# Attention probabilities turned by VectorE in 32x32 blocks and regrouped by transfers inside SBUF, in place of 128x128 transposes on TensorE

## The chip, the cores and the metric

The kernel runs on one core of a Trainium2 chip. The metric is the device time of one execution in microseconds (us), the median of several runs. A profiled execution gives a trace with the start and duration of every instruction. The engines are called PE (TensorE), DVE (VectorE), ACT (ScalarE), POOL (GpSimd) and SP (SyncE, which here issues most DMAs). Each takes its own list of instructions in order and waits on semaphores for the others.

## The reference

Block-causal attention for 8 batches of 8 heads (576 rows, head size 64, blocks of 64 rows), then a bilinear feed-forward layer over all 4608 tokens:

```python
scores = scale * np.matmul(q, k.transpose(0, 1, 3, 2))
mask = block_i >= block_j                      # blocks of 64
scores = np.where(mask, scores, -1000000000.0)
scores = scores - np.max(scores, axis=-1, keepdims=True)
attn = np.exp(scores)
attn = attn / (np.sum(attn, axis=-1, keepdims=True) + 1e-09)
x = np.matmul(attn, v)                         # heads side by side: 4608 x 512
out = ((x @ w_a) * (x @ w_b)) @ w_out          # 512 -> 1536 -> 512
```

All data is float32 (the large products run as three float32r products of high and low parts).

## The kernel before, in words

**Pairs and slots.** The 64 heads are worked in 32 pairs, and the program is a loop over slots `s` (line 576). In slot `s` three generators are advanced by the table `SLOT` (line 572): `softmax` (`S_`) of pair `s`, `turn` (`T_`) of pair `s-1`, and `values` (`V_`) of pair `s-2`, which stands first in the slot. After each step some matmuls of the first feed-forward pass (`first_pass`, called MoE matmuls below, 128x288) are put in to keep PE fed: 72 in a slot, shared out by the third numbers of the entries. They begin in slot 5. In slots 0 to 4 filler matmuls (`keep`) stand there, and the conversion of the weights (lines 141 to 212) runs on DVE and ACT.

**One pair.** The queries of a head are four tiles of 128 rows, `t` = 0 to 3, against 192, 320, 448 and 512 keys, plus a small side product for the first and the last block of queries (`e_s`, 128x128 per head). `softmax` makes the scores on PE (line 383): first tile 3, the side and tile 1, then in a second batch tiles 2 and 0. DVE takes the maxima (line 388; the two 512-wide ones of tile 3 come first in a pair), ACT the exponentials with their sums (line 391). When all are there, DVE forms the reciprocals `rc` (lines 429 to 434) and POOL scales the exponentials by them in place (line 438, ten instructions: four of tiles 3 and 2, two of the side, four of tiles 1 and 0).

**The turn.** The product with `v` needs the probabilities with the keys on the partitions. `turn` transposes them on PE against an identity (line 457), 28 transposes of 128x128 a pair into PSUM, four at a time, and ACT copies each four to SBUF (`ah`, line 460, 7 copies a pair). `values` then multiplies by `v` (line 475, `av`): per head 6 matmuls over up to 512 query columns, the two heads of the pair in the two halves of the array. DVE copies the result out (lines 484 and 485), ACT and POOL split it into high and low parts (`xh`, `xl`), and ACT's queue stores it.

**What sets the order.** PE's order is the program's order, since the loop stands in a manual schedule for PE. On the other engines the framework's scheduler decides it, so it is read from the compiled instruction lists. Of the slot's other work, the split of the next query and key into high and low parts (`q` on ACT and DVE, `k` on ACT, line 112, and POOL, line 115), and the parts of the feed-forward (`a`, `hf`, `hh`, `hl`, `ob`) share the engines.

**Buffers.** The exponentials have two sets of buffers (two pairs). PSUM has 8 banks: 2 for the MoE matmuls, 4 for scores (`ps_sc`), 2 for `tp` and `av` (`ps_t`).

Of the kernel before, what the change touches and what calls it, by code (L numbers as in the profile page):

```python
# [8 lines left out]

F32 = mybir.dt.float32  # L10
# [7 lines left out]
P = 128  # L18
BLK = 64
# [12 lines left out]
XQ = lambda nc: nc.scalar  # L32
PE_ORDER = ["PE"]
WARM = 9
KEEP = [3, 1, 1, 1, 1]
NATIVE = 6

# [17 lines left out]
def attention_then_bilinear_ffn(  # L55
# [10 lines left out]
    nc = tc.nc  # L66
    B, H, D, S = kT.shape
# [23 lines left out]
    left, right = ExitStack(), ExitStack()  # L91
# [18 lines left out]
    def split(hi, lo, src, hi_eng, lo_eng):  # L110
        if hi_eng is nc.scalar:
            nc.scalar.copy(hi, src)  # L112
        else:
            hi_eng.tensor_copy(hi, src)
        return lo_eng.tensor_tensor(lo, src, f32(hi), op=ALU.subtract)
# [43 lines left out]
    def parts(fs):  # L159
        return [(f, i) for f in fs for i in range(KP)] + [(f, KP) for f in fs]  # L160
# [53 lines left out]
    marks = []  # L214
# [72 lines left out]
    SC = slice(P * SIDE_T, P * SIDE_T + BLK), slice(P * SIDE_T + BLK, P * (SIDE_T + 1))  # L287
# [15 lines left out]

    if WARM:
        z = const.tile([P, W], F32R, name="z")
        nc.vector.memset(f32(z), 0.0)
        ps = ps_mm.tile([P, 512], F32, tag="mm", name="warm")
        for k in range(WARM):
            nc.tensor.matmul(ps, z[:, :P], z, start=True, stop=True)

    heads = {}
    xs_all = {}

    def pair_of(p):
        b, h = divmod(2 * p, H)
        return b, h, f"{b}_{h}"
# [10 lines left out]
    def load_qk(p):  # L327

        b, h, n = pair_of(p)
        take(p, "k", S, kT[b, h:h + 2].rearrange("h d s -> (h d) s"))  # L330
        take(p, "q", SQ, qT[b, h:h + 2].rearrange("h d s -> (h d) s"))

    def load_v(p):
        b, h, n = pair_of(p)
        vv = heads[p]["v"] = apool.tile([P, 2, NCH + 1, D], F32, tag="v", name=f"v{n}", bufs=3)
        for j in range(2):
            nc.sync.dma_start(vv[:, j], vm[b, h + j])
# [19 lines left out]
    rows = slice(D), slice(D, P)  # L357
# [83 lines left out]
    def turn(p):  # L441

        n = pair_of(p)[2]
        heads[p]["a"] = ah = apool.tile([P, 2, NCH, W], F32, tag="ah", name=f"ah{n}")
        for t, hs in [(t, [h]) for t in range(LAST, 0, -1) for h in range(2)] + [(0, [0, 1])]:
            tp = ps_t.tile([P, 4, P], F32, tag="tp", name=f"tp{n}_{t}_{hs[0]}", bufs=2)
            m = min(t + 2, NCH)
            todo = []
            for h in hs:
                es, e_s = e_bufs[(2 * p + h) % NE]  # L450
                todo += [es[t][:, c * P:(c + 1) * P] for c in range(m)]
                if t == SIDE_T:
                    assert m == SIDE
                    todo.append(e_s)
            m = len(todo) // len(hs)
            for c, src in enumerate(todo):
                mark = nc.tensor.transpose(tp[:, c], src, ident)  # L457
            at = slice(hs[0], hs[-1] + 1), slice(m), slice(P * t, P * (t + 1))
            got = tp[:, :len(todo)].rearrange("p (h c) n -> p h c n", h=len(hs))
            nc.scalar.copy(ah[(slice(None), *at)], got)  # L460
            yield mark

    def values(p):

        b, h, n = pair_of(p)
        t = heads.pop(p)
        hp = h // 2
        xf = xpool.tile([P, S], F32, tag="xf", name=f"xf{n}", bufs=XFB)
        av = ps_t.tile([P, W], F32, tag="tp", name=f"av{n}", bufs=2)
        av0 = ps_t.tile([P, 512], F32, tag="tp", name=f"av0{n}", bufs=2)[:, :BLK]  # L470
        v, a = t["v"], t["a"]

        def both(out, c, src, cols, start, stop):
            for i, r in enumerate(rows):
                mark = nc.tensor.matmul(  # L475
                    out[r], v[:, i, c], a[:, i, src, cols], start=start, stop=stop, skip_group_check=True)
# [5 lines left out]
        both(av[:, W - BLK:], NCH, SIDE, SC[1], False, True)  # L482
        mark = both(av0, NCH, SIDE, SC[0], True, True)
        nc.vector.tensor_copy(xf[:, BLK:], av)  # L484
# [64 lines left out]
    NP = NH // 2  # L549
    LAG = 2  # L550
# [8 lines left out]
    def want(now):  # L559

        n = (now - H - LAG) * per_slot - behind
        if now < 2 * H + LAG:
# [13 lines left out]
    for s in range(NP + LAG):  # L576
        if s == NP - 1:
            raw = fetch(wab[F1, :, 0], f"w{F1}_0")
        due = 0
        for k, (what, i, m) in enumerate(SLOT):  # L580
            i += s
            if 0 <= i < NP:
                mark = next(gens.get((what, i)) or gens.setdefault((what, i), what(i)))
                for _ in range(KEEP[s] if s < len(KEEP) else 0):
                    keep = keep or ps_mm.tile([P, 512], F32, tag="mm", name="keep")
                    nc.tensor.matmul(keep, z[:, :P], z, start=True, stop=True)  # L586
                marks.append(mark)
            if k == 0 and s < NP:
                load_v(s)
            if k == 9 and s + 1 < NP:  # L590
                split_qk(s + 1)
            if k == 9 and s + 2 < NP:
# [12 lines left out]
            while moe and n_moe < want(now):  # L605
                next(moe)
                n_moe += 1
# [146 lines left out]
    k = 0  # L754
# [8 lines left out]
    for kp in range(KP):  # L763
        g = sums_x(raw, kp, "0_0")
# [5 lines left out]
    start, pace = F2 * PER_F, STEP1  # L770
    k = 0


    for ps_ in range(2):
        fs = list(range(F1 + ps_ * F2, F1 + (ps_ + 1) * F2))
        for tt in range(NT2):
# [21 lines left out]
            todo = [(j, o) for j in (1, 0) for o in range(NO)]  # L798
            hs = {}
# [75 lines left out]
```

## Time and profile before

| | |
|---|---|
| time, median of 3 runs | 1277.9 us (1276.22 to 1278.17) |
| the profiled execution | 1277.34 us, of which the span that the trace covers is 1275.5 us |
| attention with MoE matmuls | about 110 to 660 us of the span |
| rest of the first pass, then two passes over four and four feed-forward blocks | from 660 us on |
| PE transposes (line 457) | 896 a kernel, 28 a pair |
| copies `ah` (line 460) | 224, mean 597 ns, 133.5 us of ACT |

Busy time is not the bound by itself: it says how long an engine had instructions running. To see what sets the time one asks in each stage which engine never waits, and for an engine that waits, what ends the wait. Lines of a timeline give a start, a duration, the engine and line, what is written and read, and in brackets the idle time before it and what ended it.

### The profile page before, as it was taken

What the parts mean: (1) busy time and instruction counts of PE and PEld (TensorE: products, weight loads), DVE (VectorE), ACT (ScalarE), POOL (GpSimd) and SP (SyncE); (2) the same over time, 40 slices, a digit from 0 to 9 for tenths busy, and PEclk for the clock granted to TensorE, in tenths of its full rate; (3) what the DMA queues carried; (4) which work ended last, traced back from release to release, by engine and by line L of the source; (5) the groups of instructions that cost most, each with busy time, mean ns of one, the idle gap of its engine ahead of it and who ended that gap; (6) DMA issues with size and microseconds to landing.
All of it is one profiled execution on the core that took longest, in us unless ns stands there. A gap on an engine that the chain in (4) does not pass through costs nothing.

```text
span 1275.5 us, 22228 instructions
## 1 busy us (share of the span) xinstructions
PE 1229.0 (96%) x8132; PEld 1114.6 (87%) x8132; DVE 789.1 (62%) x1932; ACT 622.8 (49%) x1550; POOL 353.5 (28%) x540
## 2 busy tenths in 40 slices
PE   6789999999999999999999899999999999999998
PEld 4556778888888888888889799999999999999998
DVE  5875444345444454444538999778778677577664
ACT  3656667576675665766645444344344223123210
POOL 2453653554535545355330020120121000000000
PEclk7888999999999999999999999999999999999999
DMA  5342222222222223221133454563578542253131
GB/s 191 107 139 72 71 77 81 96 65 74 80 88 88 65 73 97 70 88 59 35 109 95 151 119 135 153 153 95 142 192 278 161 149 85 65 149 102 47 100 62
DMA packets 68652, 135.66 MB, mean 106 GB/s; under 512 B 7616, under 2 KB 42432, under 8 KB 68544
## 3 DMA queue, kind: packets, MB, share of 16 engines
q1 hardware_dynamic: 57024, 115.37, 28.2%
q0 software_dynamic: 6912, 9.44, 4.7%
q10 hardware_dynamic: 4608, 9.44, 2.2%
q8 instruction: 64, 1.05, 0.3%
q14 instruction: 44, 0.36, 0.1%
HBM read 87.03 MB, written 47.19 MB: 105 GB/s over the span
## 4 chain that ended last, share of the span: by engine, by line
PE 74%; ACT 12%; DVE 10%; issue 3%; DMA 1%; POOL 0%; SPq 0%; ACTq 0%; DVEq 0%
PE pso_z L727 15%; PE ps L223 9%; PE psw_z L681 8%; PE psx_z L681 8%; PE psv_z L681 7%; PE av L475 7%; PE pso L223 6%; PE tp L457 5%; PE s L383 5%; ACT e L391 5%; ACT ah L460 4%; PE psy_z L681 4%; DVE nm L388 3%; ACT e_s L391 2%; PE keep L586 1%
## 5 line engine op out<-in xcount | busy, mean ns | idle before, releaser
L223 PE MATMUL ps<-xh,wab 128*128 128x288 f32 x1024 | 228.8, 305 | 0.0
L727 PE MATMUL pso_z<-h_z,wo 128*128 128x384 f32 x1152 | 203.7, 334 | 2.1 <-DVE u_z L708 2.1
L727 PEld LDWEIGHTS pso_z<-h_z,wo 128*128 128x128 f32 x1152 | 200.2, 188 | 2.5 <-issue 2.3
L438 POOL TENSOR_SCALAR e<-e,rc 128x512 f32<-128x512 f32 (+3 forms) x256 | 150.7, 611 | 161.4 <-DVE rc L434 95.2
L223 PEld LDWEIGHTS ps<-xh,wab 128*128 128x128 f32 x1024 | 168.1, 188 | 8.5 <-issue 5.2
L223 PE MATMUL ps<-xl,wab 128*128 128x288 f32 x512 | 158.0, 309 | 0.0
L460 ACT COPY ah<-tp 128x512 f32<-128x512 f32 x224 | 133.5, 597 | 41.6 <-PE tp L457 41.1
L388 DVE TENSOR_REDUCE nm<-s 128x1 f32<-128x512 f32 (+4 forms) x320 | 147.0, 484 | 9.1 <-PE s L383 6.0
L383 PE MATMUL s<-k,q 64*128 64x512 f32 (+3 forms) x900 | 118.1, 367 | 27.4 <-ACT e L391 24.7
L112 ACT CAST h_z<-u_z 128x384 fp32r<-128x384 f32 x96 | 49.3, 513 | 175.8 <-DVE u_z L706 160.2
L457 PE MATMUL tp<-ident,e 128*128 128x128 f32 x832 | 130.8, 278 | 0.1
L383 PEld LDWEIGHTS s<-k,q 64*128 64x128 f32 x900 | 78.5, 190 | 59.5 <-ACT e L391 42.8
L790 POOL DMA_DIRECT2D part<-pt x48 | 42.7, 1038 | 287.1 <-ACT pt L789 286.4
L681 PE MATMUL psx_z<-xh,wab 128*128 128x384 f32 x384 | 117.6, 342 | 3.7 <-DVE u_z L699 2.0
L681 PE MATMUL psw_z<-xh,wab 128*128 128x384 f32 x384 | 117.4, 341 | 0.0
L681 PE MATMUL psv_z<-xh,wab 128*128 128x384 f32 x384 | 116.2, 338 | 0.0
L223 PE MATMUL pso<-hh,wo 128*128 128x288 f32 x480 | 112.5, 311 | 0.8 <-ACT a L247 0.8
L457 PEld LDWEIGHTS tp<-ident,e 128*128 128x128 f32 x832 | 105.6, 143 | 5.7 <-issue 2.5
L391 ACT ACTIVATE e<-s,nm 128x448 f32<-128x448 f32 (+2 forms) x192 | 101.3, 540 | 19.0 <-DVE nm L388 18.9
L484 DVE COPY xf<-av 128x512 f32<-128x512 f32 x32 | 22.1, 691 | 130.4 <-PE av L475 130.4
L475 PE MATMUL av<-ah,v 128*64 128x64 f32 (+4 forms) x768 | 93.6, 393 | 6.6 <-ACT ah L460 4.5
L223 PEld LDWEIGHTS ps<-xl,wab 128*128 128x128 f32 x512 | 96.4, 188 | 1.6 <-issue 0.4
(114 smaller groups left out, 2323.4 us busy)
## 6 DMA issues: line engine op xcount, KB each, us to landing
xr<-xd SPq DMA_DIRECT2D x48, 384.0 KB, 3.9
raww<-wab SPq DMA_DIRECT2D x24, 512.0 KB, 3.9
v<-vm SPq DMA_DIRECT2D x64, 160.0 KB, 3.4
xd<-xf ACTq DMA_DIRECT2D x32, 288.0 KB, 2.6
part<-ob SPq DMA_DIRECT2D x64, 144.0 KB, 2.0
part<-pt POOLq DMA_DIRECT2D x48, 192.0 KB, 7.3
pt<-part SPq DMA_DIRECT2D x48, 192.0 KB, 3.2
outT<-pt SPq DMA_DIRECT2D x48, 192.0 KB, 3.3
```

The costliest lines, as they stand in the source:

```text
L112: nc.scalar.copy(hi, src)
L223: mm = nc.tensor.matmul(ps, w_, d_, start=(i == 0), stop=(i == n - 1))
L383: mark = nc.tensor.matmul(outs[h], qq[r, q0[t]:q0[t] + P], keys, start=j == 0, stop=j == len(qk) - 1)
L388: nc.vector.tensor_reduce(nm[:, h, t:t + 1], view, axis=AX.X, op=ALU.max, negate=True)
L391: nc.scalar.activation(out, view, AF.Exp, bias=bias, accum_out=sm[:, h, t, :1])
L438: nc.gpsimd.tensor_scalar(ev, ev, rc[:, h, t:t + 1], 1.0, op0=ALU.mult, op1=ALU.mult)
L457: mark = nc.tensor.transpose(tp[:, c], src, ident)
L460: nc.scalar.copy(ah[(slice(None), *at)], got)
L475: mark = nc.tensor.matmul(out[r], v[:, i, c], a[:, i, src, cols], start=start, stop=stop, skip_group_check=True)
L681: nc.tensor.matmul(ps, wt[:, i, iw], j[:, ix], start=start and kp == 0 and i == 0 and j is xh, stop=kp == KP - 1 and i == 1, skip_group_ch ...
L727: nc.tensor.matmul(ps, wt[:, a, osl], b, start=i == 0, stop=i == 3 * len(fs) - 1)
L790: nc.gpsimd.dma_start(part[o * P:(o + 1) * P, ts], t, accum_op=ALU.add)
```

## The change

What `turn` does is replaced. DVE transposes each exponential tile in blocks of 32x32 (line 453 of the new file, `STREAM_TRANSPOSE`, 8 a pair, 128 partitions by 512, 512, 384 and 256 elements for each head) and the four 64x64 pieces of the side that are used (line 458). The blocks land in one buffer `bl`. Such a transpose stays within a group of 32 partitions, so 16 DMAs on SP (line 463), each of 32 partitions with 3584 bytes apiece, move the blocks to the partition group where their keys belong, into one buffer `at`. There are no transposes on PE, no identity and no `ah` copies.

`values` reads `at` in pieces of 128 (or 64) queries: 15 matmuls a head in place of 6, over the same 1600 columns. It stands at the end of slot `p+1` in place of the start of slot `p+2`. The copies of its result go from DVE to ACT (lines 487 and 488). All 8 PSUM banks less the two for MoE serve scores and `av` in one ring of 6. `SLOT` has new shares for the same 72 MoE matmuls of a slot: 31 now stand between the two batches of scores and 41 between the second batch and `av`. `v` of a pair is loaded by one DMA, not two.

```diff
-    ps_sc = psum(right, "ps_sc", 4)
-    ps_t = psum(right, "ps_t", 1)
-    ident = const.tile([P, P], F32, name="ident")
-    make_identity(nc, ident)
+    ps_sc = psum(right, "ps_sc", 6)
...
+    at_e = [sum(ew[:t]) // P for t in range(NT)]
+    NE_ = sum(ew) // P + 1
+    bl = const.tile([P, NQ, 2, NE_, QB], F32, name="bl")
+    nc.gpsimd.memset(bl[:, :, :, NE_ - 1], 0.0)
...
-            for c, src in enumerate(todo):
-                mark = nc.tensor.transpose(tp[:, c], src, ident)
-            at = slice(hs[0], hs[-1] + 1), slice(m), slice(P * t, P * (t + 1))
-            got = tp[:, :len(todo)].rearrange("p (h c) n -> p h c n", h=len(hs))
-            nc.scalar.copy(ah[(slice(None), *at)], got)
-            yield mark
+        for t in (*range(LAST, 0, -1), 0):
+            for h in range(2):
+                es, e_s = e_bufs[(2 * p + h) % NE]
+                nc.vector.transpose(blocks(h, slice(at_e[t], at_e[t] + ew[t] // P), slice(P)),
+                                    es[t].rearrange("p (c g q) -> p c g q", g=NQ, q=QB))
+                if t == SIDE_T:
+                    for i in range(2):
+                        r = slice(BLK * i, BLK * (i + 1))
+                        nc.vector.transpose(bl[r, :BLK // QB, h, NE_ - 1],
+                                            e_s[r, r].rearrange("p (g q) -> p g q", q=QB))
+                yield None
+        for i in range(NQ):
+            for g in range(NQ):
+                nc.sync.dma_start(at[QB * g:QB * (g + 1), i], bl[QB * i:QB * (i + 1), g])
+        yield None
...
-            a0 = max(P * c - BLK, 0)
-            both(av[:, a0:], c, c, slice(a0, W), c == 0, False)
+            for t in range(max(c - 1, 0), NT):
+                first = NQ // 2 if c == t + 1 else 0
+                both(av[:, P * t + QB * first:P * (t + 1)], c, at_e[t] + c, slice(first, NQ), c == t == 0, False)
...
-        nc.vector.tensor_copy(xf[:, BLK:], av)
-        nc.vector.tensor_copy(xf[:, :BLK], av0)
+        nc.scalar.copy(xf[:, BLK:], av)
+        nc.scalar.copy(xf[:, :BLK], av0[:, :BLK])
...
-    SLOT = [(V_, -2, 0), (*S1, 6), (*S1, 5), (*T1, 5), (*S1, 5), (*T1, 5), (*S1, 5), (*T1, 6),
-            (*S1, 6), (*S1, 5), (*T1, 5), (*S1, 5), (*T1, 5), (*S1, 5), (*T1, 5), (*T1, 4)]
+    SLOT = [(*S1, 8), (*T1, 0), (*S1, 8), (*T1, 0), (*T1, 0), (*S1, 8), (*T1, 0), (*T1, 0), (*S1, 8),
+            (*T1, 0), (*T1, 0), (*T1, 0), (*T1, 0), (*S1, 9), (*S1, 9), (*S1, 9), (*S1, 13), (V_, -1, 0)]
```

Three places in the compiled lists matter below. The first is **DVE**, where one pair ends and the next begins, in a slot with MoE matmuls. Of the change before it (`rc_2` is the reciprocal of the ending pair, `xf` the copy of an earlier pair's result, `nm_4` from `s_4` the first maxima of the next pair):

```order
L434 RECIPROCAL rc_2_4189<-rc_2_4189 128x10
L484 COPY xf_0_4428<-av_0_4429 128x512
L485 COPY xf_0_4428<-av_0_4430 128x64
L388 TENSOR_REDUCE nm_4_4457<-s_4_0_4460 128x1
L388 TENSOR_REDUCE nm_4_4457<-s_4_1_4461 128x1
```

and now:

```order
L435 RECIPROCAL rc_2_4196<-rc_2_4196 128x10
L458 STREAM_TRANSPOSE bl<-e_s 64x2x32 x4
L453 STREAM_TRANSPOSE bl<-e_3_117 128x4x4x32
L453 STREAM_TRANSPOSE bl<-e_3_125 128x4x4x32
L453 STREAM_TRANSPOSE bl<-e_2_116 128x4x4x32
L453 STREAM_TRANSPOSE bl<-e_2_124 128x4x4x32
L453 STREAM_TRANSPOSE bl<-e_1_115 128x3x4x32
L453 STREAM_TRANSPOSE bl<-e_1_123 128x3x4x32
L453 STREAM_TRANSPOSE bl<-e_0_114 128x2x4x32
L453 STREAM_TRANSPOSE bl<-e_0_122 128x2x4x32
L389 TENSOR_REDUCE nm_4_4467<-s_4_0_4470 128x1
```

All twelve transposes of the ending pair stand between its reciprocals and the first maximum of the next pair, the four of the side ahead of the others, although the program spreads the calls over the next pair's softmax. In every second slot an `hf` of the feed-forward stands among the four of the side.

The second place is **POOL**, around the first scaling instructions of a pair. Before (`rc_2` is pair p, `rc_4` pair p+1, `k_6` the key of a later pair, `xl` and `hl` low parts):

```order
L438 TENSOR_SCALAR e_0_122<-e_0_122,rc_2_2045 128x192
L438 TENSOR_SCALAR e_0_130<-e_0_130,rc_2_2045 128x192
L115 TENSOR_TENSOR k_6_2195<-kr_6_2196,k_6_2195 128x576
L115 TENSOR_TENSOR xl_0_0_2302<-xf_0_2284,xh_0_0_2301 128x288
L115 TENSOR_TENSOR xl_0_1_2306<-xf_0_2284,xh_0_1_2305 128x288
```

and now:

```order
L115 TENSOR_TENSOR xl_6_0_4185<-xf_6_4149,xh_6_0_4184 128x288
L115 TENSOR_TENSOR xl_6_1_4189<-xf_6_4149,xh_6_1_4188 128x288
L115 TENSOR_TENSOR hl_0_0_4285<-hf_0_0_4282,hh_0_0_4284 128x288
L115 TENSOR_TENSOR k_6_4356<-kr_6_4357,k_6_4356 128x576
L439 TENSOR_SCALAR e_3_117<-e_3_117,rc_2_4196 128x512
L439 TENSOR_SCALAR e_3_125<-e_3_125,rc_2_4196 128x512
```

The split of the later key, which stood behind the scaling of `rc_2`, now stands ahead of it. In the other slots one `hl` stands between the first and the second scaling instruction as well.

The third place is **SP**, with the loads for a later pair (`kr`, `qr`, `v`) and stores of the feed-forward (`ob`). Before:

```order
L325 DMA kr_4_7285<-kT 128x576
L507 DMA part<-ob_3_7173 128x288
L337 DMA v_2_7401<-vm 128x320 x2
L325 DMA qr_6_7559<-qT 128x640
L325 DMA kr_6_7556<-kT 128x576
```

and now, with the 16 transfers of a pair (`at_2`):

```order
L327 DMA kr_0_4625<-kT 128x576
L327 DMA qr_0_4628<-qT 128x640
L338 DMA v_4_4735<-vm 128x640
L463 DMA at_2_4515<-bl 32x896 x16
L327 DMA kr_2_4900<-kT 128x576
L327 DMA qr_2_4903<-qT 128x640
```

The first of the 16 waits for the last transpose, so the loads behind it wait with it.

More of the change, by code (lines that the diff above doesn't have):

```diff
@@ L6 @@
 from concourse import mybir
-from concourse.masks import make_identity
 from concourse._compat import with_exitstack
@@ L34 @@
 WARM = 9
+ATB = 1
 KEEP = [3, 1, 1, 1, 1]
@@ L335, in load_v @@
         vv = heads[p]["v"] = apool.tile([P, 2, NCH + 1, D], F32, tag="v", name=f"v{n}", bufs=3)
-        for j in range(2):
-            nc.sync.dma_start(vv[:, j], vm[b, h + j])
+        nc.sync.dma_start(vv, vm[b, h // 2])
     def parts_of(p, tag):
@@ L443, in turn, with blocks @@
         n = pair_of(p)[2]
[L444 to L449, printed above, removed]
+        heads[p]["a"] = at = apool.tile([P, NQ, 2, NE_, QB], F32, tag="at", name=f"at{n}", bufs=ATB)
+        def blocks(h, e_, part_):
+            return bl[part_, :, h, e_].rearrange("p g c q -> p c g q")
@@ L463, in values @@
+                yield None
[3 more added lines that the diff above has]
+        yield None
     def values(p):
         b, h, n = pair_of(p)
-        t = heads.pop(p)
+        t_ = heads.pop(p)
         hp = h // 2
         xf = xpool.tile([P, S], F32, tag="xf", name=f"xf{n}", bufs=XFB)
-        av = ps_t.tile([P, W], F32, tag="tp", name=f"av{n}", bufs=2)
-        av0 = ps_t.tile([P, 512], F32, tag="tp", name=f"av0{n}", bufs=2)[:, :BLK]
@@ L471, in values, with both @@
[L471 to L476, printed above, removed]
+        av, av0 = (ps_sc.tile([P, 512], F32, tag="sc", name=f"av{i}{n}") for i in range(2))
+        v, a = t_["v"], t_["a"]
+        def both(out, c, e_, qs, start, stop):
+            for h, d in enumerate(rows):
+                mark = nc.tensor.matmul(out[d], v[:, h, c], a[:, qs, h, e_], start=start, stop=stop,
+                                        skip_group_check=True)
@@ L486, in values @@
+        both(av[:, W - BLK:], NCH, NE_ - 1, slice(NQ // 2, NQ), False, True)
+        mark = both(av0[:, :BLK], 0, NE_ - 1, slice(NQ // 2), True, True)
+        nc.scalar.copy(xf[:, BLK:], av)
+        nc.scalar.copy(xf[:, :BLK], av0[:, :BLK])
         xs = []
@@ L583, in attention_then_bilinear_ffn @@
                 mark = next(gens.get((what, i)) or gens.setdefault((what, i), what(i)))
-                for _ in range(KEEP[s] if s < len(KEEP) else 0):
+                for _ in range(KEEP[s] if m and s < len(KEEP) else 0):
                     keep = keep or ps_mm.tile([P, 512], F32, tag="mm", name="keep")
                     nc.tensor.matmul(keep, z[:, :P], z, start=True, stop=True)
-                marks.append(mark)
-            if k == 0 and s < NP:
+                if mark is not None:
+                    marks.append(mark)
+            if what is V_ and s < NP:
                 load_v(s)
-            if k == 9 and s + 1 < NP:
+            if k == 14 and s + 1 < NP:
                 split_qk(s + 1)
-            if k == 9 and s + 2 < NP:
+            if k == 14 and s + 2 < NP:
                 load_qk(s + 2)
@@ L858 @@
         "kT": flat(k.transpose(0, 1, 3, 2)),
-        "vm": flat(np.concatenate([v[:, :, : NCH * P], v[:, :, :BLK], v[:, :, NCH * P:]], axis=2)
-                   .reshape(B, H, NCH + 1, P, D).transpose(0, 1, 3, 2, 4)),
+        "vm": flat(np.concatenate([v, v[:, :, NCH * P:]], axis=2)
+                   .reshape(B, H // 2, 2, NCH + 1, P, D).transpose(0, 1, 4, 2, 3, 5)),
         "wab": flat(np.stack([wb[:, :, 0::2], wa[:, :, 0::2], wa[:, :, 1::2], wb[:, :, 1::2]], axis=3)
```

11 lines of the change are left out of this document (3 added, 8 removed).

## Prediction, made before the changed kernel ran

> **What bounds the kernel now.** First the page, then the busy time by stretches, the chain that ended last, and the waits.
>
> ```profile
> span 1275.5 us, 22228 instructions
> PE 1229.0 (96%) x8132; PEld 1114.6 (87%) x8132; DVE 789.1 (62%) x1932; ACT 622.8 (49%) x1550; POOL 353.5 (28%) x540
> ...
> 129.70:641.70 512.00, 501.82 (x3973) 427.88 (x3973) 231.71 (x785) 332.28 (x957) 250.41 (x392) 1.00 0.24 77
> ...
> 129.73 2.92 PE av L475 x24
> ...
> 641.72 2.92 PE av L475 x24
> ...
> DVE xf L484 <- PE av L475: 130.4, 29, 6.5
> ```
>
> The third row is the attention with MoE matmuls: columns PE, PEld, DVE, ACT, POOL, then granted clock, DMA share and GB/s. PE works 501.8 of 512 us at clock 1.00, the others 45, 65 and 49%. Between the `av` at 129.73 and that at 641.72 lie 26 pairs, so a pair takes 512.0/26 = **19.69 us**, 19.3 of them PE work. DVE waits longest for PE (last row). In this stage PE is last, and every wait of the others is cover.
>
> **What the change takes from PE and gives it.**
>
> ```profile
> 469.33 0.60 PE L457 MATMUL tp<-ident,e 128*128 128x128 f32 x4
> 469.69 0.38 PE L223 MATMUL ps<-xl,wab 128*128 128x288 f32 x1
> ...
> L475 PE MATMUL av<-ah,v 128*64 128x64 f32 x256 | 12.8, 221 | 0.0
> ```
>
> Matmuls overlap, so I go by start to start: four transposes take 0.36 us, the 7 groups of a pair 2.5 us. `av` streams the same columns in 60 records (each fp32 matmul leaves two) instead of the 24 that took 2.92 us. By the 64-column records (12.8/256 = 0.05 us each) 60 take 3.0 us; by 2.92/24 each 7.3 us. I take 3.2, since the columns are the same. PE work falls to 19.3 - 2.5 + 0.3 = **17.1 us** a pair (21.2 at the other end). ACT loses the seven `ah` copies and gains the result copies (0.9 us). If PE stayed last, 27 pairs would give back 27 x 2.6 = 70 us.
>
> **What it puts on DVE.** By the DVE list of the change all transposes of a pair stand between its reciprocals and the next pair's first maxima, and they wait for POOL's scaling. That makes a loop from pair to pair. Its parts, from the slot at 467 us:
>
> ```profile
> 467.24 1.29 DVE L388 TENSOR_REDUCE nm<-s 128x1 f32<-128x512 f32 x2 [0.17 <-PE s L383]
> ...
> 479.40 0.22 DVE L434 RECIPROCAL rc<-rc 128x10 f32<-128x10 f32 x1
> 486.09 0.69 DVE L484 COPY xf<-av 128x512 f32<-128x512 f32 x1 [6.48 <-PE av L475]
> ...
> 471.24 0.58 ACT L460 COPY ah<-tp 128x512 f32<-128x512 f32 x1
> ...
> 472.70 0.62 ACT L460 COPY ah<-tp 128x512 f32<-128x512 f32 x1
> ...
> 473.54 0.60 ACT L460 COPY ah<-tp 128x512 f32<-128x512 f32 x1
> ...
> 475.89 0.64 ACT L391 ACTIVATE e<-s,nm 128x448 f32<-128x448 f32 x1 [0.72 <-DVE nm L388]
> ...
> 478.74 0.22 ACT L391 ACTIVATION_READ_ACCUMULATOR e<-s,nm 128x1 f32 x1
> ...
> 479.30 0.71 ACT L112 CAST k<-kr 128x576 fp32r<-128x576 f32 x1
> ...
> 473.72 0.80 POOL L115 TENSOR_TENSOR hl<-hf,hh 128x288 fp32r<-128x288 f32 x1 [4.16 <-ACT hh L112]
> 479.71 2.61 POOL L438 TENSOR_SCALAR e<-e,rc 128x512 f32<-128x512 f32 x4 [5.19 <-PE tp L457]
> 482.28 0.73 POOL L438 TENSOR_SCALAR e_s<-e_s,rc 128x128 f32<-128x128 f32 x2
> 482.98 1.86 POOL L438 TENSOR_SCALAR e<-e,rc 128x320 f32<-128x320 f32 x4
> 484.78 1.43 POOL L115 TENSOR_TENSOR k<-kr,k 128x576 fp32r<-128x576 f32 x1
> ```
>
> Call E the end of a pair's last exponential (478.74 + 0.22 = 478.96). (1) POOL's split of a key now stands ahead of the scaling and needs ACT's cast, which follows the exponentials directly: E + 0.6, and 1.43 on POOL gives E + 2.0; today scaling begins 0.75 us after E. (2) Four scalings take 2.57 us to the start of the side's, the two sides 0.73: the first side is scaled at E + 4.95, the second at E + 5.3, and DVE, which has the side first, idles until then. (3) Four small transposes, about 0.13 us each, two of them hidden: E + 5.6. (4) Eight large ones. The trace has no DVE transpose. The nearest row is the DVE instruction of the same width, the 512-wide maximum: two take 1.29 us, 0.6 from start to start; the narrower widths scaled give 0.5 and 0.42, so 2 x (0.6 + 0.6 + 0.5 + 0.42) = 4.3 us, and the pair ends at **E + 9.9**. (5) Then the next pair's first maxima, and from there to its E: today 467.24 to 478.96, 11.7 us, less three `ah` copies that ACT now doesn't make in between (about 0.47 each): **10.3** (9.6 if the idle 0.72 before the 448-wide exponential, which came from late scores, goes too). The loop is 9.9 + 10.3 = 20.2 us. In every second slot an `hl` (0.80) stands in POOL's scaling and an `hf` (about 0.4) among DVE's side transposes: 21.4. The mean, **20.8 us**, is more than today's 19.69 and than PE's 17.1. The stall that goes (PE's) has this one behind it.
>
> What is queued behind DVE's wait: maxima of tile 3, so ACT's exponentials, so the PSUM banks for the scores of tile 0 (PE waits there), and `hf`, which frees a MoE bank. PE's work of a pair ends about 3.7 us early, and covers a dearer `av` up to 6.9 us.
>
> **Sum for this stage.** From pair 4 to pair 31 are 27 loops: 27 x (20.8 - 19.69) = **+30 us**.
>
> **The 16 transfers.** 16 x 114,688 bytes = 1.835 MB a pair; no row has a transfer inside SBUF.
>
> ```profile
> q1 hardware_dynamic: 57024, 115.37, 28.2%
> ...
> part<-ob SPq DMA_DIRECT2D x64, 144.0 KB, 2.0
> ...
> wabd<-st SPq DMA_DIRECT2D x8, 896.0 KB, 5.5
> ...
> 480.34 1.21 SPq L507 DMA_DIRECT2D part<-ob  x2
> 478.17 0.33 SPq L507 DMA_DIRECT2D part<-ob  x1
> ```
>
> From below: the packets of q1 took 28.2% of 16 engines for 115.37 MB, 3.1 us per MB, so 5.7 us spread over all engines, or 16 issues at 0.33 = 5.3, plus one landing of 2.0: about 8. From above: 16 landings of 2.0 one after another, 32. I take 11, by the 896 KB row twice (it is the size nearest to half a pair). `av` comes after 41 MoE matmuls and the second scores, at about E + 2.6 of the next pair, 13.5 us after the last transpose; with PE's 3.7 us of slack nothing waits up to about 16 us. Cost: 0. Without that cover, at D us for the transfers, the next pair's first transpose (E + 5) waits for `bl`, and the loop is D + 5.3. The loads behind them on SP are for later pairs and have a slot to spare.
>
> [...]
>
> **The first slots.** There DVE converts weights as well.
>
> ```profile
> 88.97 1.21 DVE L147 SCALAR_TENSOR_TENSOR mw<-raww,mw 128x512 f32<-128x512 uint16 x1
> ...
> 90.50 0.22 DVE L434 RECIPROCAL rc<-rc 128x10 f32<-128x10 f32 x1
> ...
> 95.96 1.19 DVE nm L388 x2
> ...
> 637.12 0.20 ACT L391 ACTIVATION_READ_ACCUMULATOR e<-s,nm 128x1 f32 x1
> ...
> 657.59 2.93 PE av L475 x24
> ```
>
> From reciprocal to next maxima lie 5.2 us, with conversion in them. In the new list this stretch holds the wait for scaling (3.3), the transposes (4.6) and four conversion steps (about 2.6): 10.5, so +5.3, less 1 for the result copies that go to ACT, and less some conversion that moves out of the rest of the slot. I take +3 for five pairs: **+15 us** (0 to +25). The end of attention: the last `av` comes some 23 us after the last E in both (the last two rows, 637.3 to 660.5; now 9.9 + 11 + 3), so 0. `v` in one DMA and the identity's removal: 0, behind the first weight load.
>
> **Sum:** against the profiled execution, 1275.5 + 1.8 outside its span = 1277.3; 1277.3 + 30 + 15 = 1322. The median is 0.6 above that execution. I say **1322**, 1295 to 1350 by step 4 and the first slots.
>
> **Rivals.**
>
> *Transposes cheap (faster).* DVE has cheaper rows of this width:
>
> ```profile
> L145 DVE TENSOR_SCALAR mw<-raww 128x512 int32<-128x512 int32 x36 | 15.5, 430 | 0.3
> ```
>
> That one starts its successor after 0.33 us. At that rate the eight cost 2.2 us instead of 4.3, and with the 0.7 of step 5 the loop is 18.0: 27 x (18.0 - 19.69) = -46, and +5 early: 1237. The sign turns where loop and first slots cancel, at about 19.3 us a pair. The floor is PE's 17.1, 1277 - 70 + 5 = 1212. [...] Chance 0.23.
>
> *Transposes dear.* At twice the 4.3 us (the 512-wide step at 88.97 took 1.21 us) the loop is 25.1: 27 x 5.4 + 25 = +171, 1448. Chance 0.08.
>
> *Transfers last.* At D = 18 the loop is 23.3: 27 x 3.6 + 15 = +112, 1390. It decides from D = 16. Chance 0.13.
>
> *The forecast*, DVE's loop last at 20 to 21.5 us: 0.56.
>
> [...]
>
> **Range and chances.** The low end cuts the cheap case about in half, the high end takes in the transfers at 18 us: 1240 to 1395. A measurement of this kernel tells about 0.2% (2.6 us) from no change. Slower: 0.56 + 0.08 + 0.13, less 0.04 for loops near today's: 0.73. Same 0.04, faster 0.23.
>
> **What would show it.** In the changed profile: DVE idle before the side's transposes, released by POOL `e_s`, some 4 us a pair; the eight transposes at 0.4 to 0.6 us each behind it; PE waiting for exponentials or `hf`, busy about 82% of that stage; pairs 20 to 21.5 us apart, `av` not released by a DMA. Wrong: `av` waiting for DMA (third rival), transposes near 0.3 us or 1.2 us (first, second), or PE still 98% busy.

## The result and the profile after

| | before | after |
|---|---|---|
| time, median (4 runs each) | 1277.06 us | 1341.3 us |
| ratio, 95% interval | | 1.0509 (1.0484 to 1.0533) |
| profiled execution, span | 1275.5 us | 1342.7 us |
| reciprocals of pair 0 to pair 4 | 82.2 us | 83.0 us |
| pair 4 to pair 5 | 17.8 us | 23.5 us |
| a pair, pair 4 to pair 31 | 19.58 us | 22.13 us |
| a pair, pair 5 to pair 31 | 19.65 us | 22.08 us |
| last reciprocals to the end of the span | 637.3 us | 633.8 us |

The change is 5% slower. The difference of the spans, 67.2 us, lies almost wholly in the attention with MoE matmuls. A pair's reciprocals `rc` are a good mark, since they come right after its last exponential. These are those of the pairs 4, 5 and 31 in the timeline of the kernel before (start, duration, engine, line):

```profile
109.50 0.22 DVE L434 RECIPROCAL rc<-rc 128x10 f32<-128x10 f32 x1
...
127.28 0.22 DVE L434 RECIPROCAL rc<-rc 128x10 f32<-128x10 f32 x1
...
638.15 0.21 DVE L434 RECIPROCAL rc<-rc 128x10 f32<-128x10 f32 x1
```

and, after, of the pairs 0, 4, 5 and 31:

```profile
28.22 0.22 DVE L435 RECIPROCAL rc<-rc 128x10 f32<-128x10 f32 x1
...
111.23 0.21 DVE L435 RECIPROCAL rc<-rc 128x10 f32<-128x10 f32 x1
...
134.70 0.22 DVE L435 RECIPROCAL rc<-rc 128x10 f32<-128x10 f32 x1
...
708.86 0.22 DVE L435 RECIPROCAL rc<-rc 128x10 f32<-128x10 f32 x1
```

Between pair 4 and pair 31 lie 27 pairs: (638.15 - 109.50)/27 = 19.58 before, (708.86 - 111.23)/27 = 22.13 after, so 27 x 2.55 = **+69.0 us** there. The first slots have +1.7 (111.23 less 109.50), the rest -3.5. The first of the 27, from pair 4 to pair 5, is not like the others: in the changed kernel seven conversion steps (5.8 us) still run on DVE there, and it is 5.7 us longer. The 26 pairs behind it have 26 x 2.43 = 63.3 us.

Busy time after, from the page, the view by stretches (130 to 630 us; PE, PEld, DVE, ACT, POOL, granted clock, DMA share, GB/s), and the waits of that stretch (total us, times, longest):

```profile
PE 1170.9 (87%) x8357; PEld 1103.8 (82%) x8357; DVE 907.5 (68%) x2254; ACT 531.3 (40%) x1390; POOL 344.9 (26%) x537
...
L458 DVE STREAM_TRANSPOSE bl<-e_s 64x64 f32<-64x64 f32 x128 | 27.2, 230 | 131.7 <-POOL e_s L439 123.1
```

```profile
130.00:630.00 500.00, 408.27 (x3652) 373.30 (x3652) 285.09 (x903) 228.22 (x723) 220.92 (x344) 0.88 0.57 154
...
PE av L477 <- DMA at<-bl: 1.1, 1, 1.1
```

PE, which waited under 5 us of these 500 before, is busy 408 of them, at a mean granted clock of 0.88. No engine is full any more: a loop through several engines sets the pair. DVE waits 123 us in front of the side's transposes for POOL. `av` waits for a transfer once.

The chain of work that ended last shows the loop, here one whole round of it, from one pair's large transposes to the next pair's (start, duration, what; "issue" is time in which nothing shown was waited for):

```profile
471.30 4.06 DVE bl L453 x8
475.37 1.17 DVE nm L389 x2
...
477.91 1.45 ACT e L392 x4
479.36 0.30 ACT a L247
...
479.70 2.29 PE pso L223 x8
481.99 1.46 PE s L384 x4
...
483.67 1.12 DVE nm L389 x2
...
486.55 0.82 ACT e L392 x4
487.36 0.57 ACT k L112
...
488.06 1.44 POOL k L115
489.50 2.56 POOL e L439 x4
492.07 0.70 POOL e_s L439 x2
...
493.43 4.06 DVE bl L453 x8
...
501.77 1.32 PE ps L223 x8
```

(The last row belongs to the next round.) The round is 493.43 - 471.30 = 22.1 us long and passes DVE, ACT, PE, DVE, ACT, POOL, DVE. Two stretches of it: from the last exponential (E, 487.36) to the last transpose (497.49) 10.1 us, in every other pair 11.2; and from there to the next E 10.8 to 12.0 (475.36 to 487.36 is 12.0, 497.49 to 508.27 is 10.8). The means over 25 pairs are 10.6 and 11.5.

The second stretch has something that the prediction did not: `a`, and MoE matmuls on PE, on the chain. The timeline shows what they are, and the view by stretches (columns as above) the granted clock:

```profile
475.43 11.16 SPq L463 DMA_DIRECT2D at<-bl  x16
...
477.91 0.69 ACT L392 ACTIVATE e<-s,nb 128x512 f32<-128x512 f32 x1 [5.16 <-DVE nb L412]
...
479.70 0.61 PE L223 MATMUL pso<-hh,wo 128*128 128x288 f32 x1 [3.91 <-ACT a L247]
```

```profile
479.70:486.20 6.50, 6.50 (x29) 5.91 (x30) 3.64 (x13) 4.01 (x15) 0.80 (x1) 0.50 0.66 154
501.80:503.10 1.30, 1.30 (x10) 1.13 (x10) 1.12 (x5) 1.06 (x6) 0.27 (x1) 1.00 0.80 185
```

31 MoE matmuls stand on PE ahead of the second scores. After 23 of them PE needs a bank that ACT frees with the copy `a` (line 247). In ACT's list `a` stands behind the exponentials of tile 3, and these wait 5.16 us for DVE (`nb`, behind the transposes). So PE stands still for 3.91 us. Then it works for 6.5 us at a granted clock of 0.50: the 8 MoE matmuls that are left take 2.29 us on the chain. Only then come the second scores, and DVE has waited 2.21 us for them. In the next round PE stands still for 3.31 us at the same place; there the clock is still 1.00 when it begins again, the 8 matmuls take 1.32 us, and the half clock comes 1.5 us later, under the scores. Between 130 and 630 us the trace has 22 gaps of PE of 2.45 to 4.84 us, 19 of them for `a`, and around the end of each the granted clock falls to 0.50, for 3.4 or 6.8 us. The fall begins between 2.3 us before PE goes on and 1.5 us after; what sets its begin and its length is not shown by any run.

### The profile page after: what moved, and what is told of

Its sections match the earlier page's. It is cut to its first block, busy times and chain, and to the rows that moved or that the text cites. A ratio compares the mean times of both kernels' runs of the same rounds, so it can differ in the third digit from the quotient of the medians.

```text
span 1342.7 us, 23315 instructions
## 1 busy us (share of the span) xinstructions
PE 1170.9 (87%) x8357; PEld 1103.8 (82%) x8357; DVE 907.5 (68%) x2254; ACT 531.3 (40%) x1390; POOL 344.9 (26%) x537
## 4 chain that ended last, share of the span: by engine, by line
PE 47%; DVE 19%; issue 10%; ACT 9%; POOL 9%; DMA 3%; SPq 2%; DVEq 0%; POOLq 0%; ACTq 0%
PE pso_z L731 14%; DVE bl L453 9%; PE psv_z L685 7%; PE psx_z L685 7%; PE psw_z L685 7%; ACT e L392 6%; DVE nm L389 6%; POOL e L439 4%; PE psy_z L685 3%; PE s L384 3%; PE ps L223 3%; POOL k L115 3%; PE pso L223 3%; DMA v<-vm 2%; SPq L463 1%
## 5 line engine op out<-in xcount | busy, mean ns | idle before, releaser
L223 PEld LDWEIGHTS ps<-xh,wab 128*128 128x128 f32 x1024 | 178.3, 200 | 62.3 <-ACT a L247 45.4
L384 PE MATMUL s<-k,q 64*128 64x512 f32 (+3 forms) x900 | 126.2, 416 | 33.4 <-ACT e L392 27.3
L439 POOL TENSOR_SCALAR e<-e,rc 128x512 f32<-128x512 f32 (+3 forms) x256 | 145.4, 586 | 36.8 <-DVE rc L435 36.8
L384 PEld LDWEIGHTS s<-k,q 64*128 64x128 f32 x900 | 91.9, 234 | 61.2 <-ACT e L392 33.7
L223 PEld LDWEIGHTS pso<-hh,wo 128*128 128x128 f32 x480 | 89.9, 216 | 61.1 <-ACT a L247 52.4
L453 DVE STREAM_TRANSPOSE bl<-e 128x512 f32<-128x512 f32 (+2 forms) x256 | 130.5, 575 | 0.9 <-POOL e L439 0.4
L477 PEld LDWEIGHTS av<-at,v 128*64 128x64 f32 x1920 | 102.0, 149 | 31.4 <-issue 19.0
L477 PE MATMUL av<-at,v 128*64 128x128 f32 (+1 forms) x1920 | 106.3, 274 | 24.0 <-DMA at<-bl 22.6
L458 DVE STREAM_TRANSPOSE bl<-e_s 64x64 f32<-64x64 f32 x128 | 27.2, 230 | 131.7 <-POOL e_s L439 123.1
L223 PEld LDWEIGHTS ps<-xl,wab 128*128 128x128 f32 x512 | 102.7, 201 | 6.4 <-POOL xl L115 5.0
```

The lines of the kernel that those rows point to most:

```text
L223: mm = nc.tensor.matmul(ps, w_, d_, start=(i == 0), stop=(i == n - 1))
L384: mark = nc.tensor.matmul(outs[h], qq[r, q0[t]:q0[t] + P], keys, start=j == 0, stop=j == len(qk) - 1)
L439: nc.gpsimd.tensor_scalar(ev, ev, rc[:, h, t:t + 1], 1.0, op0=ALU.mult, op1=ALU.mult)
L453: nc.vector.transpose(blocks(h, slice(at_e[t], at_e[t] + ew[t] // P), slice(P)), es[t].rearrange("p (c g q) -> p c g q", g=NQ, q=QB))
L477: mark = nc.tensor.matmul(out[d], v[:, h, c], a[:, qs, h, e_], start=start, stop=stop, skip_group_check=True)
```

## The experiments

All are edits of the changed kernel but one. "A pair" is worked out as above, from pair 4 and from pair 5 to pair 31; the last two columns are means over 25 pairs of the two stretches (E to the last transpose, and from there to the next E). From pair 4 to pair 5, where conversion still runs, most of the edited kernels take 24 to 31 us. So the steady pair is the one from pair 5 on; the two stretches add up to it within 0.1 us.

| run | edit | time, us | ratio to before (95%) | pairs 0 to 4 | a pair, 4 to 31 | a pair, 5 to 31 | to last T | to next E |
|---|---|---|---|---|---|---|---|---|
| changed | | 1341.3 | 1.0509 (1.0484 to 1.0533) | 83.0 | 22.13 | 22.08 | 10.6 | 11.5 |
| e1 | no transfers | 1264.0 | one run | 65.8 | 19.84 | 19.80 | 9.3 | 10.6 |
| e2 | key's split behind scaling | 1303.5 | 1.0219 (1.0185 to 1.0254) | 83.1 | 20.67 | 20.42 | 9.5 | 10.9 |
| e3 | second scores early | 1282.7 | 1.0039 (1.0021 to 1.0057) | 82.9 | 19.85 | 19.68 | 10.7 | 9.1 |
| e4 | maxima first | 1503.2 | one run | 99.7 | 27.36 | 27.33 | | |
| e5 | maxima first, `av` later | 1291.0 | 1.0116 (1.0086 to 1.0145) | 74.5 | 20.17 | 20.06 | | |
| e6 | large transposes first | 1286.9 | 1.0081 (1.0060 to 1.0102) | 78.8 | 20.02 | 19.68 | 9.0 | 10.7 |
| e7 | e2 + e3 + e6 | 1267.7 | 0.9923 (0.9908 to 0.9939) | 78.9 | 19.40 | 19.04 | 10.0 | 9.2 |
| e9 | e6, no transfers | 1268.0 | one run | 68.0 | 19.86 | 19.82 | 9.3 | 10.6 |
| e10 | e7, a quarter issued by ACT | 1322.4 | 1.0371 (1.0345 to 1.0397) | 84.0 | 21.24 | 20.91 | 9.4 | 11.6 |
| e11 | before, no turn of pairs 0 to 3 | 1280.0 | one run | 83.3 | 19.51 | 19.63 | | |
| e12 | e2 + e6 | 1276.3 | 0.9990 (0.9972 to 1.0008) | 79.1 | 19.78 | 19.44 | 9.0 | 10.4 |
| e13 | e7 with 21 MoE matmuls ahead | 1274.6 | 0.9982 (0.9969 to 0.9995) | 78.7 | 19.84 | 19.42 | 9.1 | 10.2 |

### e2: one link of the loop

```diff
-        split(hi, lo, raw, nc.scalar, nc.gpsimd)
+        behind_of(split(hi, lo, raw, nc.scalar, nc.gpsimd), "scaled")
```

(`behind_of` orders an instruction behind the last scaling instruction on POOL, without a wait.)

> POOL's split of the next key is ordered behind the scaling, in place of ahead of it. Theory (every link of the loop costs one for one): from the last exponential to the first large transpose 6.1 and 7.2 us become 4.7 and 5.8, 27 x 1.35 = 36 us less, 1305 us. Rival (the loop has slack at POOL, something on PE's side is last): 1338 to 1344 us, with DVE's wait for POOL shorter and another wait longer by as much.

Measured 1303.5 us, 37.8 less. The first stretch fell by 1.1 us (1.35 expected), so the loop has no slack at POOL. The second stretch fell by 0.6 as well, which the sum of links doesn't give; a steady pair is 1.66 shorter. Between 130 and 630 us PE waits 57 us for `a` in place of 76, and its mean granted clock is 0.94 in place of 0.88. That fits the second stretch, but no run takes it alone.

### e3: the second stretch

```diff
-    SLOT = [(*S1, 8), (*T1, 0), (*S1, 8), ... (*S1, 8), ... (*S1, 8), ...
-            (*S1, 9), (*S1, 9), (*S1, 9), (*S1, 13), (V_, -1, 0)]
+    SLOT = [(*S1, 3), (*T1, 0), (*S1, 3), ... (*S1, 3), ... (*S1, 3), ...
+            (*S1, 14), (*S1, 14), (*S1, 15), (*S1, 17), (V_, -1, 0)]
```

> 12 in place of 31 MoE matmuls stand between the two batches of scores, 60 in place of 41 behind the second. Theory (the step that I sized too small, first maxima to last exponential, is long because PE, ahead of the second batch, waits for the copy a that stands behind the exponentials on ACT, and then runs MoE matmuls at half clock): that step falls from 11.6 to about 10.3 us, 27 x 1.3 = 35 us less, 1306 us. Rival (the step is long on DVE and ACT by itself, PE's wait is cover): within 5 us of 1341. A rival on the other side (the 60 behind delay av and the next first scores past the transposes' end): slower than 1345.

Measured 1282.7 us, 58.6 less. The same marks of pairs 4 and 31:

```profile
110.31 0.21 DVE L435 RECIPROCAL rc<-rc 128x10 f32<-128x10 f32 x1
...
646.21 0.20 DVE L435 RECIPROCAL rc<-rc 128x10 f32<-128x10 f32 x1
```

A pair takes 19.85 us, 2.28 less (from pair 5 on 19.68, 2.40 less). The first stretch stayed (10.7), the second fell from 11.5 to 9.1: all of the gain is in the step that I had too small, and it fell further than expected. The work is the same, only PE's order is another; PE's waits for `a` fell from 76 us of the 500 to 2. So what made the stretch long was PE standing ahead of the second scores. The run does not take apart how much of it is the wait, how much the slow clock behind it, and how much the plain time of what stood there: 19 matmuls fewer are some 3 us even at the full clock, by the 8 that took 1.32 us. e12 and e13 say that the wait alone is not all. With the first stretch shorter, 21 matmuls ahead in place of 31 took the waits for `a` from 35 us to 1, and the second stretch only from 10.4 to 10.2.

### e1, e6 and e9: the transfers in the steady stage

e1 leaves the 16 transfers out (`av` reads a buffer that is set to zero once):

```diff
-        for i in range(NQ):
-            for g in range(NQ):
-                nc.sync.dma_start(at[QB * g:QB * (g + 1), i], bl[QB * i:QB * (i + 1), g])
         yield None
```

> The 16 transfers of each pair are left out; av reads a buffer that is set to zero once, so the output is not the attention's. Theory (the loop DVE transposes -> first maxima -> exponentials -> POOL scaling sets the pair, the transfers lie beside it): pairs stay at 22.1 us from pair 4 to 31, and the time falls only by what the first slots wait for transfers, 1330 to 1341 us. Rival (the transfers are last: av waits for them, or the transposes wait for the buffer they read): pairs fall by 2 us or more, to 20 us or less, 1290 us or less.

1264.0 us, pairs of 19.84 (19.80 from pair 5): as the rival has it. But the lists show that the scheduler, without the transfers, also put the large transposes ahead of the side's. They then run while POOL still scales, and the first stretch is 1.3 us shorter. Two things changed, so e1 decides nothing. e6 takes that order with the transfers, e9 the same without them:

```diff
+                if t >= SIDE_T:
+                    behind_of(tr, "tr")
+                    last["tr"] = tr
...
-                        nc.vector.transpose(bl[r, :BLK // QB, h, NE_ - 1], ...
+                        behind_of(nc.vector.transpose(bl[r, :BLK // QB, h, NE_ - 1], ...), "tr")
```

> The changed kernel with DVE's large transposes of tiles 3, 2 and 1 ordered ahead of the side's, as the run without transfers had them; the transfers are all there. That run came to 1264 us with pairs of 19.84 us, so it also had another order of transposes, which speaks for neither theory. Theory (the loop; transfers beside it): the large transposes now run while POOL still scales, from the last exponential to the last transpose 10.6 us become 9.3, pairs 22.1 - 1.4 = 20.7 (down to 19.9 as in the run without transfers), 27 x 1.4 to 2.2: 1282 to 1303 us. Rival (the transfers were what the run without them saved): pairs stay above 21.8, 1335 us or more.

> The kernel with the large transposes first, and its 16 transfers of a pair left out (av reads a buffer set to zero once, so the output is not the attention's); the lists of DVE, ACT and POOL are the same in the stage with MoE matmuls, but for hf. Theory (transfers are hidden there): the same time a pair as with the transfers, within 0.3 us; what they cost lies in the first slots, where the run without them took 65.8 us for four pairs and the changed kernel 83.0. Rival: pairs shorter by 1 us or more than with the transfers.

The marks of pairs 5 and 31 in e6, then in e9:

```profile
135.47 0.22 DVE L435 RECIPROCAL rc<-rc 128x10 f32<-128x10 f32 x1
...
647.07 0.22 DVE L435 RECIPROCAL rc<-rc 128x10 f32<-128x10 f32 x1
```

```profile
122.19 0.20 DVE L437 RECIPROCAL rc<-rc 128x10 f32<-128x10 f32 x1
...
637.40 0.22 DVE L437 RECIPROCAL rc<-rc 128x10 f32<-128x10 f32 x1
```

In the steady stage e6 has (647.07 - 135.47)/26 = 19.68 us a pair, e9 19.82. So what e1 saved a pair there was the order; the transfers are not seen to cost anything. The spans differ by 1282.2 - 1266.2 = 16.0 us all the same: 13.3 up to pair 5, -3.6 from there to pair 31, and 6.3 behind it, where nothing covers the last pair's transfers (the last `av` of e6 waits 5.46 us for them). The 13.3 up to pair 5 can't be put down to the transfers alone: in e9's first slots DVE's list has another order, with the 512-wide maxima last. In e6, from pair 4 to pair 5 a conversion step waits for a weight load, which SP issues behind a pair's transfers and the loads that follow them:

```profile
121.73 0.43 DVE L141 TENSOR_SCALAR sw<-raww 128x512 int32<-128x512 int32 x1 [5.17 <-DMA raww<-wo]
```

e6's gain of 2.4 us a steady pair is above the 1.4 that I gave the order; 0.8 of it is in the second stretch, again not followed up.

### e4 and e5: is it the place of the transposes?

Both order all transposes of a pair behind the next pair's first maxima:

```diff
+                behind_of(tr, "nb")
```

e5 also moves `av` behind the next first batch of scores (and lets the MoE matmuls begin 0.2 slots later, since they need its result):

```diff
-    SLOT = [(*S1, 8), (*T1, 0), ... (*S1, 13), (V_, -1, 0)]
+    SLOT = [(*S1, 8), (V_, -2, 0), (*T1, 0), ... (*S1, 13)]
```

> The changed kernel with all transposes of a pair behind the next pair's first maxima on DVE, and av left where the change has it. Theory (the transfers take some 13 us and are hidden only because av stands a slot behind the transposes): the cover is gone, transposes (7.7 us from nb to their end) + 12.6 to 13 of transfers + av 3 + scores 1.2 + maxima 2.9 make a loop of 27 us, 1440 to 1500 us, PE waiting 5 us or more a pair for DMAs ahead of av. Rival (the place of the transposes alone sets the pair): as the run with av later, 20 us a pair, 1280 to 1300.

> All transposes of a pair are ordered behind the next pair's first maxima (nb) on DVE, and av of the pair is moved a third of a slot later, behind the next first batch of scores, so that the transfers keep the time they had. The work is the same. Theory (the place of the transposes costs, not they themselves): the next exponentials no longer wait for POOL's scaling and the transposes, the pair falls from 22.1 to 18 to 19.5 us and PE is 88 to 95% busy there: 1341 - 27 x 3.3 = 1250 us (1225 to 1290). Rival (the transposes load DVE, or their reads and writes and the transfers slow the others, wherever they stand): 1320 us or more.

e4 took 1503.2 us, just above the 1440 to 1500 expected. Its chain, from the last transposes of one pair to the `av` of the next:

```profile
450.35 0.77 DVE bl L453 x2
...
451.71 0.58 SPq L464
...
460.61 2.26 DMA at<-bl
462.92 5.08 PE av L478 x56
...
490.48 4.94 PE av L478 x56
```

`av` to `av` is 27.6 us (27 was expected). The transfers take 462.87 - 451.12 = 11.8 us from the last transpose to the last landing, and here all of it is on the path. What hid them is the place of `av`, a slot behind.

e5 took 1291.0 us, pairs of 20.17: less than the changed kernel's 22.13, but not the 18 to 19.5 expected. Its waits from 130 to 630 us:

```profile
PE av L478 <- DMA at<-bl: 38.2, 14, 3.8
```

The exponentials are out of the loop, and the next one shows: in more than half of the pairs `av` waits for the transfers, though it was moved back for them. This is the sign that the prediction gave for its third rival, and it comes true as soon as the first loop is open. (DVE's transposes wait for no DMA in e5.)

### e7, e12 and e13: how far the edits add

> Three edits together: large transposes first, the key's split behind the scaling, 12 in place of 31 MoE matmuls ahead of the second scores. Theory: 19.85 us a pair (second scores early) less 1.35 (key) less 1.4 (order) is 17.1, which is where PE's work (17.1) becomes last: 17.3 to 18 us a pair, 1283 - 27 x 2.2 = 1224 us (1210 to 1240), faster than the kernel before. Rival (with the loop this short the transfers become last: 13 us from the last transpose to the last landing, and transposes of the next pair wait for their buffer): pairs at 18.5 us or more, 1247 us or more, with DVE waiting for a DMA ahead of its transposes or PE ahead of av.

> Large transposes first and the key's split behind the scaling, with the changed kernel's shares of MoE matmuls. Theory (links of the loop add): pairs of 20.0 us (large first alone) less 1.2 for the key: 18.8, 1287 - 33 = 1254 us. Rival (transfers are last at this length: 13 us from the last transpose to the last landing plus 5 of transposes is 18, and what else stands in the queues comes on top): 19.2 us a pair or more, 1265 us or more.

> As the kernel of three edits, with 21 in place of 12 MoE matmuls ahead of the second scores. Theory: between the kernels with 31 and with 12 of them, and shorter than both if what held the latter (a product hf ahead of the transposes on DVE waiting for PE's MoE matmuls, 3 us in every second slot) moves off the transposes: 18.5 to 19.0 us a pair, 1245 to 1258 us. Rival (transfers last): 19.2 us or more, 1263 us or more.

```diff
-    SLOT = [(*S1, 3), (*T1, 0), (*S1, 3), ... (*S1, 3), ... (*S1, 3), ...
-            (*S1, 14), (*S1, 14), (*S1, 15), (*S1, 17), (V_, -1, 0)]
+    SLOT = [(*S1, 5), (*T1, 0), (*S1, 5), ... (*S1, 5), ... (*S1, 6), ...
+            (*S1, 12), (*S1, 12), (*S1, 12), (*S1, 15), (V_, -1, 0)]
```

(That is e13 against e7.) e7 comes to **1267.7 us, 0.9923 of the kernel before: faster than both**, but not the 1224 of the theory. All three stop at 19.0 to 19.4 us a steady pair, as their rivals have it. In e7's timeline:

```profile
439.27 5.57 SPq L466 DMA_DIRECT2D at<-bl  x7
...
446.93 2.95 DVE L453 STREAM_TRANSPOSE bl<-e 128x512 f32<-128x512 f32 x5 [4.09 <-DMA part<-ob]
...
465.45 0.46 DVE L249 TENSOR_TENSOR hf<-ps,a 128x288 f32<-128x288 f32 x1 [3.13 <-PE ps L223]
```

In one slot the transposes wait 4.09 us for `bl`, whose last seven transfers are issued until 444.84 and land until 446.55 (the row names the stores behind them); in the next an `hf` stands ahead of them and waits 3.13 us for PE. In e12 the same wait is there:

```profile
DVE bl L453 <- DMA part<-ob: 23.9, 6, 5.0
...
DVE bl L453 <- DMA at<-bl: 18.4, 7, 6.6
```

`bl` is a single buffer, so the next transposes wait until the transfers have read it: 44 us of the 500 in e7, in 12 waits, and 42 in e12. In e7 the waits of `hf` for PE are as large, 44 us, so the transfers are one of two that are last there. A second buffer `bl` was not tried.

### e10: can the transfers be issued faster?

```diff
-                nc.sync.dma_start(at[...], bl[...])
+                q = nc.scalar if i == NQ - 1 else nc.sync
+                q.dma_start(at[...], bl[...])
```

> The kernel of the three edits (1267.7 us, pairs of 19.4, in which every second pair's transposes waited 4 us for their buffer, which 16 transfers issued 0.64 us apart on one queue were still reading), with 4 of the 16 transfers issued by ACT, which idles there. Theory (the issues one after another on SP set how long the transfers take): they take 4 x 0.64 = 2.6 us less, the wait in every second pair falls from 4.1 to about 1.5 us, 27 x 1.3 = 35 us less at most, 1235 to 1255 us. Rival (the bytes set it, 1.835 MB at some 180 GB/s): the issues on each queue spread out and the last landing comes as late as before, 1262 us or more. A rival on the other side: ACT's exponentials wait behind the four issues, slower than 1270.

1322.4 us: the rival on the other side. Its timeline, the issues on both queues and ACT's next exponential:

```profile
448.16 11.06 SPq L467 DMA_DIRECT2D at<-bl  x12
...
448.45 3.45 ACTq L467 DMA_DIRECT2D at<-bl  x3
...
474.00 0.69 ACT L392 ACTIVATE e<-s,nb 128x512 f32<-128x512 f32 x1 [5.76 <-DMA at<-bl]
```

12 issues on SP take as long (11.06 us) as 16 did in the changed kernel (11.16), and three on ACT 3.45. The second queue took nothing off; it held ACT's exponentials, for 5.76 us in the slot shown, and the second stretch grew from 9.2 to 11.6 us. So the issuing on SP alone is not the limit; what the two queues share was not taken apart.

### e11: the first slots

The kernel *before*, with the transposes and copies of pairs 0 to 3 left out (`ah` is set to zero).

```diff
+        if p < 4:
+            nc.gpsimd.memset(ah, 0.0)
...
+            return
```

> The kernel before, with the transposes and copies of the first four pairs left out (their transposed probabilities are set to zero, so those heads' output is not the attention's). Theory (the first slots of before were as much PE's as DVE's: its transposes took 0.85 us for each four there, 6 us a pair, so that taking them away paid for what the change put on DVE, which I had added at +15): the four pairs from the first to the fifth reciprocal fall from 82.3 to 62 to 74 us. Rival (DVE's conversion is last there): 79 us or more.

From the first to the fifth reciprocals it took 115.41 - 32.14 = 83.3 us, where 82.2 was with them and the theory had 62 to 74: taking PE's transposes and ACT's copies away shows no gain there. The run is not clean: POOL sets `ah` to zero instead, 3.5 us a pair, two of them in this stretch.

## Why the prediction was right, and where it was wrong

The forecast was slower, by DVE's loop, at 1322 us in a range of 1240 to 1395; 1341.3 came. The mechanism was the one forecast, and it set the pair; its terms were partly off.

- **Steps 1 to 4, right.** E + 9.9 and 11.1 were forecast for the end of the transposes, 10.1 and 11.2 came; POOL's scaling began at E + 2.1 (2.0), the eight large transposes took 4.06 us (4.3), DVE's wait ahead of the side's 4.4 to 4.8 (some 4). The value for the transposes came from the maxima of the same width, and it held; so neither cheap nor dear transposes.
- **Step 5, too small: 10.3 forecast, 11.5 measured.** What failed is the deduction in "today 11.7, less three `ah` copies". From first maxima to E the stretch did not get shorter at all. These rows have the second scores in the kernel before, then the first maxima and the second scores in the changed one:

```profile
474.13 1.66 PE L383 MATMUL s<-k,q 64*128 64x448 f32 x12
```

```profile
475.29 1.25 DVE L389 TENSOR_REDUCE nm<-s 128x1 f32<-128x512 f32 x2
...
481.92 2.07 PE L384 MATMUL s<-k,q 64*128 64x448 f32 x12
```

  Before, the second scores come 474.13 - 467.24 = 6.9 us after the first maxima, and E 4.8 us after them; now 6.6 and 487.36 - 481.92 = 5.4. (The means over 24 pairs are 6.85 and 4.78, then 6.21 and 5.43: 11.6 both times.) PE sets when the second scores come. Before, it gets there without a pause; in the new loop it waits for `a`, behind exponentials which the loop itself delays, and then runs at half clock (0.50 from 479.70 us on). So it was of little use to take copies from ACT. I had written that PE's slack covers what waits there, and looked at the end of the pair, not at the second scores inside it. e3 shows that PE's order decides: with the scores earlier the stretch is 9.1 us. The step is 26 x 1.2 = 31 of the 34 us by which the 26 steady pairs exceed the forecast (+63 for +29); steps 1 to 4 have the other 26 x 0.13 = 3.4.
- **The first slots, too large: +15 forecast, +1.7 measured up to pair 4, +7.4 up to pair 5.** The stretch from reciprocals to the next first maxima grew, in the slot behind pair 2 from (before)

```profile
68.17 0.22 DVE L434 RECIPROCAL rc<-rc 128x10 f32<-128x10 f32 x1
...
73.10 0.68 DVE L388 TENSOR_REDUCE nm<-s 128x1 f32<-128x512 f32 x1
```

  4.9 us to (after)

```profile
66.63 0.22 DVE L435 RECIPROCAL rc<-rc 128x10 f32<-128x10 f32 x1
...
77.46 1.28 DVE L389 TENSOR_REDUCE nm<-s 128x1 f32<-128x512 f32 x2
```

  10.8 us (10.5 forecast). But the rest of the slot fell from 22.3 - 4.9 = 17.4 to 21.9 - 10.8 = 11.1 us, where I had given back 2.3. Over the four slots the stretches have +15.2 us and the rests -14.4. About half of that is conversion: between the reciprocals of pairs 0 and 4 DVE spends 31.1 us on 48 steps in place of 38.3 on 53, and seven steps come only behind pair 4. What made the other half shorter is open: e11 shows no gain from leaving out PE's transposes. The four pairs take 68.0 us in e9 and 78.8 in e6, but DVE's order differs there too.
- **The transfers, right, with less to spare than forecast.** 11 us were taken from the last transpose to the last landing; in the changed kernel it is 12.2 on average (11.7 to 13.6), in e4's chain 11.8. They were to be hidden up to 16; `av` began 2.2 us after the last landing on average, so the cover was some 14.4. It sufficed: `av` waited 1.1 us in the stage, and a steady pair of e6 takes no more time than one of e9. That rival was rightly kept: the transfers hold up e5, e7, e12 and e13. The 1.835 MB of a pair took 10.0 to 11.8 us of issues in the changed kernel, 155 to 183 GB/s.
- **The end, 0 forecast, -3.5 us measured.** The last `av` ends 26.9 us after the last reciprocals in place of 22.4, since it waits 6.9 us for the last transfers, which nothing covers. The passes behind it are 8.1 us shorter; this was not followed up.

The total came out 19 us above the forecast in part because errors cancelled: the stage from pair 4 on is 39 us over, the first slots and the end 17 under.

PE's floor of 17.1 us a pair (1212 us) was reached by no run.

## What to carry to other kernels

When the bound moves from one full engine to a loop through several, a stretch copied from the old trace holds only if nobody in it waits for a new place in another engine's list: follow each queue inside it, and ask what a late copy holds up. Shortening such a loop pays only until the next one shows, here the transfers, for which `av` and the single buffer wait; so work out the second loop before promising what opening the first is worth. And an experiment that leaves work out may make a scheduler reorder what is left: compare the lists before reading its time. Last, begin a mean over pairs where the stage is steady: in e6 one slot of 28.8 us among 27 made steady pairs of 19.68 us look like 20.02.

## What was not expected of the hardware

A transfer of 32 partitions by 3584 bytes inside SBUF was issued each 0.64 us (0.59 and 0.05 between them in the chain of e4), where most loads on the same queue took 0.33 to 0.43 in the changed kernel, and splitting the 16 over two queues left the total at 11 us (11.06 in place of 11.16). After an idle gap of PE of 3.31 us, the granted clock fell from 1.00 to 0.50 only 1.5 us after the matmuls had gone on. On DVE a blockwise float32 transpose of 128x512 took what a maximum over as many elements did, 680 and 665 ns on average in the changed kernel: eight of 512 to 256 wide take 4.06 us, as against 4.3 worked out from maxima.
